# Attention with pooled queries, two MLPs on one core: row sums inverted in PSUM, a weight's sign added as a signed zero, transfers of a pair spread over its steps

## Chip, core and metric

The kernel runs on one core of a Trainium2 chip. The metric is the time of one execution on the device in microseconds, as the median of several runs. The core has TensorE (matrix products and transposes), VectorE, ScalarE and GpSimd for elementwise work, and SyncE, which here issues most of the transfers; 16 DMA engines move the data. In rows of the profile these are PE, DVE, ACT, POOL and SP.

## What is computed

```python
def _attn_ref(q, k, v):                      # batch 2, heads 8, seq 1152, head_dim 64
    q_pool = q.reshape(B, H, S // 2, 2, D).mean(axis=3)
    scores = scale * np.matmul(q_pool, k.transpose(0, 1, 3, 2))
    scores = scores - np.max(scores, axis=-1, keepdims=True)
    attn = np.exp(scores)
    attn = attn / (np.sum(attn, axis=-1, keepdims=True) + 1e-09)
    return np.matmul(attn, v).astype(np.float32)
...
x = np.ascontiguousarray(attn_out.transpose(0, 2, 1, 3)).reshape(B * S, H * D)   # 1152 x 512
x = _moe_ref(x=x, **moe_kwargs)              # (h * tanh(softplus(h))) @ w_out, h = x @ w_in, 512 -> 2048 -> 512
return _moe2_ref(x=x, **moe2_kwargs)         # 8 experts 512 -> 1024 -> 512, ReLU, weighted by 8 Sinkhorn rounds
```

The weights `w_in` and `w_out` of the first MLP arrive as float64, read as int64; all else is float32. Products are made of two float32r parts, high and low, of each operand.

## The kernel before

Three stages follow each other: attention (0 to about 265 us), the first MLP, and the experts. The change is in the first.

**Attention** goes through 8 pairs of heads. Each pair has 9 tiles of 128 query rows, so there are 72 steps `g` in one loop, and `p, t = divmod(g, 9)` gives the pair and the place `t` in it (0 to 8). In step `g`, TensorE makes the scores of tile `g` into the single PSUM tile `psS` (6 matmuls; 12 at place 4, whose tile holds rows of both heads, from `qz`). VectorE takes them out with a running minimum (L483). ScalarE makes the exponentials with their row sum (L497). SyncE copies the exponentials of tile `g - 1` into a buffer `er` of another type, 576 KB (`hand_over`, L503); there are two such buffers. TensorE transposes tile `g - 3` out of `er` in 9 transposes of 128x128 (`psT`, L560); ScalarE (L563) and VectorE (L566) split the result into high and low parts `eth` and `etl`; and TensorE multiplies them with V (`psA`, L581). The PSUM pool `ps_t` has four buffers in turn; `psT`, `psk`, `psq` and `psr` share them.

What else happens in a pair, by tables and lists in the code:

- `TURN` says at which place the transposes of K (`psk`) and Q (`psq`) are made for the next or the same pair. Q comes in three parts: u = 0 at place 6 for the next pair, u = 1 at place 1 and u = 2 at place 0. After each, `swap` has SyncE copy one half of the partitions to the other (`qT`, 2 x 128 KB, or `qz`, 2 x 64 KB). Part u = 2 is first read by the scores of place 4, u = 1 by those of place 5.
- `row_sums` at place 0 of the next pair adds 1e-9 to the 128x9 row sums and inverts them on VectorE; `turn_sums` at place 1 transposes them to 9x128 (`psr`), VectorE copies them out (`rt`, L515), SyncE writes them to DRAM (`row`, L520) and reads them back with a broadcast in three transfers (`rx`, L526). GpSimd multiplies the finished sums with `rx` (L607).
- The list `first` holds what SyncE must issue at the start of the next step, ahead of that step's `hand_over`. Each engine and SyncE work off their instructions in order, so a transfer that waits holds up what is behind it.
- GpSimd's queue loads and splits q, k and v (`prep`).
- `load_w` prepares the weights of the MLP. Six tiles of 128x512 float64 values (512 KB each, `raw`) are prepared within attention, marked `busy`; each is planned at five times `ts` counted in steps `g`. SyncE loads `raw` 2.4 stages of 2 steps ahead of `ts[0]`; there the high words are scaled by 2^-112 on GpSimd (L149) and the low words converted on ScalarE (L153). VectorE shifts and masks each half of a tile (L160) at `ts[1]` and two steps later, and puts the sign into it (L169) one step after each. GpSimd then joins high and low word (L175) and splits the result.

## Time and profile before

| | |
|---|---|
| median of 3 runs | 1220.34 us (1220.3 to 1220.45) |
| the profiled execution | 1223.26 us |
| its span, first to last instruction | 1221.5 us |
| busy in the span: TensorE, VectorE, ScalarE, GpSimd | 1203.7, 855.8, 592.1, 654.0 us |
| busy share of TensorE | 99% |
| granted TensorE clock | 1.000 (full speed) over the span |

The busy time of an engine is the time in which the profile shows an instruction on it; matmuls are pipelined and their ends are modelled, so that short waits of TensorE may be seen as busy. The time of an execution is a little longer than its span, and an execution under the profiler a little longer than one without.

### The profile page before, as it was taken

The numbers are of one execution on the slowest core, as the hardware profiler recorded it, in microseconds if no ns is written. First come the engines' busy times: TensorE is split into PE (matmuls) and PEld (weight loads), VectorE is DVE, ScalarE is ACT, GpSimd is POOL, SyncE is SP. The second block draws the span as 40 slices with busy tenths as digits, with TensorE's granted clock in tenths as the row PEclk, the third lists the DMA queues.
The fourth block names the chain that finished last, engine by engine and source line by source line (L and its number), as shares of the span: only waits on it lengthen the run. The fifth ranks groups of instructions, "written<-read, shape, count | busy, mean of one in ns | idle before, by whom it ended". The sixth has DMA issues, their size and how long they took to land.

```text
span 1221.5 us, 19362 instructions
## 1 busy us (share of the span) xinstructions
PE 1203.7 (99%) x6840; PEld 1110.4 (91%) x6840; DVE 855.8 (70%) x1598; ACT 592.1 (48%) x1354; POOL 654.0 (54%) x752
## 2 busy tenths in 40 slices
PE   8899999999999999999999999999999999999998
PEld 8899999999999999898888889999888889999887
DVE  7899999876444333787866677766866777866865
ACT  7888889877544443543332233333333233333331
POOL 7667777415444331485755566555555565555551
PEclk9999999999999999999999999999999999999999
DMA  6787787653223210011111111111011111111112
GB/s 202 265 281 263 272 264 255 232 179 120 88 71 98 74 31 30 1 52 53 32 38 45 52 48 49 52 52 52 23 40 52 53 44 52 53 52 38 37 39 78
DMA packets 51985, 116.39 MB, mean 95 GB/s; under 512 B 7977, under 2 KB 22897, under 8 KB 51889
## 3 DMA queue, kind: packets, MB, share of 16 engines
q1 hardware_dynamic: 48400, 103.36, 25.9%
q0 software_dynamic: 3488, 11.80, 3.3%
q8 instruction: 54, 0.88, 0.3%
q14 instruction: 43, 0.34, 0.1%
HBM read 66.86 MB, written 2.40 MB: 57 GB/s over the span
## 4 chain that ended last, share of the span: by engine, by line
PE 90%; DVE 5%; DMA 4%; ACT 1%; issue 1%; POOL 0%; POOLq 0%; ACTq 0%
PE po L1237 30%; PE c L1067 26%; PE ph L231 10%; PE po L806 8%; PE psS L478 4%; PE psA L581 4%; DMA er<-e 4%; PE psT L560 3%; DVE e L483 2%; DVE etl L566 1%; PE psk L410 1%; PE psw L646 0%; ACT eth L563 0%; PE pg L861 0%; PE psq L456 0%
## 5 line engine op out<-in xcount | busy, mean ns | idle before, releaser
L83 POOL TENSOR_TENSOR wslotsl<-s,wslotsh 128x256 fp32r<-128x256 f32 x180 | 132.0, 743 | 237.1 <-ACT wslotsh L76 237.1
L1245 DVE SCALAR_TENSOR_TENSOR oacc<-po,Pm,oacc 128x512 f32<-128x512 f32 (+1 forms) x217 | 161.1, 746 | 102.2 <-PE po L1237 95.8
L1237 PE MATMUL po<-wdbl,hhall 128*128 128x512 f32 (+1 forms) x543 | 214.4, 395 | 0.0
L1237 PE MATMUL po<-wdbh,hlall 128*128 128x512 f32 (+1 forms) x543 | 214.1, 394 | 0.0
L1237 PE MATMUL po<-wdbh,hhall 128*128 128x512 f32 (+1 forms) x543 | 214.0, 394 | 0.0
L1084 ACT ACTIVATE t<-c 128x384 f32<-128x384 f32 x80 | 39.3, 491 | 246.2 <-PE c L1067 246.2
L1104 ACT ACTIVATE hhall<-c 128x384 fp32r<-128x384 f32 x180 | 88.6, 492 | 127.4 <-DVE c L1100 124.7
L1237 PEld LDWEIGHTS po<-wdbh,hhall 128*128 128x128 f32 x543 | 102.1, 188 | 24.3
L1237 PEld LDWEIGHTS po<-wdbl,hhall 128*128 128x128 f32 x543 | 102.1, 188 | 23.3
L1237 PEld LDWEIGHTS po<-wdbh,hlall 128*128 128x128 f32 x543 | 102.1, 188 | 23.2
L83 POOL TENSOR_TENSOR wslotsl<-rawu,wslotsh 128x256 fp32r<-128x256 f32 x120 | 90.9, 772 | 49.8 <-ACT wslotsh L76 49.8
L483 DVE TENSOR_SCALAR_CACHE_REDUCE e<-psS 128x1152 f32<-128x1152 f32 x72 | 97.3, 1352 | 22.0 <-PE psS L478 11.7
L566 DVE TENSOR_TENSOR etl<-psT,eth 128x384 fp32r<-128x384 f32 (+1 forms) x240 | 108.0, 507 | 4.8 <-ACT eth L563 4.2
L563 ACT ACTIVATE eth<-psT 128x384 fp32r<-128x384 f32 (+1 forms) x240 | 92.8, 477 | 15.6 <-PE psT L560 15.2
L1105 DVE SCALAR_TENSOR_TENSOR hlall<-c,hhall 128x384 fp32r<-128x384 f32 x180 | 98.7, 548 | 2.1
L1067 PE MATMUL c<-x2l,wslotsh 128*128 128x384 f32 x280 | 94.3, 337 | 0.0
L1067 PE MATMUL c<-x2h,wslotsl 128*128 128x384 f32 x280 | 94.1, 336 | 0.0
L1067 PE MATMUL c<-x2h,wslotsh 128*128 128x384 f32 x280 | 93.8, 335 | 0.0
L497 ACT ACTIVATE e<-e,nm 128x1152 f32<-128x1152 f32 x70 | 89.3, 1276 | 0.1
L175 POOL TENSOR_TENSOR wt<-wt,raw 128x512 int32<-128x512 int32 x32 | 42.4, 1325 | 84.0 <-DVE wt L169 59.8
L478 PE MATMUL psS<-kT,qT 128*128 128x384 f32 x384 | 81.9, 348 | 2.8 <-DVE e L483 2.7
L76 ACT ACTIVATE wslotsh<-s 128x256 fp32r<-128x256 f32 x180 | 72.0, 411 | 24.3 <-DVE s L1033 24.3
(365 smaller groups left out, 3117.2 us busy)
## 6 DMA issues: line engine op xcount, KB each, us to landing
er<-e SPq DMA_DIRECT2D x70, 576.0 KB, 4.1
rawd<-in_moe_w_dram SPq DMA_DIRECT2D x60, 256.0 KB, 2.7
rawu<-in_moe_w_dram SPq DMA_DIRECT2D x30, 384.0 KB, 3.3
raw<-in_moe_w_in_dram SPq DMA_DIRECT2D x16, 512.0 KB, 4.3
raw<-in_moe_w_out_dram SPq DMA_DIRECT2D x16, 512.0 KB, 3.7
vraw<-in_v_dram POOLq DMA_DIRECT2D x15, 288.0 KB, 4.7
kraw<-in_k_dram POOLq DMA_DIRECT2D x13, 288.0 KB, 4.6
qT<-qT SPq DMA_DIRECT2D x28, 128.0 KB, 3.1
```

Of the source, the lines that this page charges most:

```text
L83: eng.tensor_tensor(out=lo, in0=src, in1=hi.bitcast(F32), op=ALU.subtract)
L231: nc.tensor.matmul(ps[:, 0:TH], lhsT=a, rhs=b, start=(n == 0), stop=(n == len(ops) - 1))
L478: nc.tensor.matmul(ps[:, kb, 0:TH], lhsT=a, rhs=kt[:, kb * TH:(kb + 1) * TH], start=(n == 0), stop=(n == len(ops) - 1))
L483: nc.vector.tensor_scalar(sc, ps[:, :, 0:TH], -1.0, None, op0=ALU.mult, op1=ALU.min, accum_out=nm)
L497: nc.scalar.activation(e, sc, AF.Exp, bias=nm, scale=-1.0, accum_out=rsS[p][:, t:t + 1])
L563: nc.scalar.activation(eh[:, cs, o:o + b - a], ps[:, 0:3, a:b], AF.Copy)
L566: nc.vector.tensor_tensor(out=el[:, cs, o:o + b - a], in0=ps[:, 0:3, a:b], in1=eh[:, cs, o:o + b - a].bitcast(F32), op=ALU.subtract)
L806: nc.tensor.matmul(ps[:, 0:TH], lhsT=a, rhs=b, start=(n == 0), stop=(n == len(ops) - 1))
L1067: nc.tensor.matmul(cb[c], lhsT=a_, rhs=b_, start=FIRST[n] and m == 0, stop=LAST[n] and m == len(ops) - 1, skip_group_check=True)
L1105: los.append(lambda: nc.vector.scalar_tensor_tensor(out=lo, in0=b, scalar=0.0, in1=hi.bitcast(F32), op0=ALU.max, op1=ALU.subtract))
L1237: nc.tensor.matmul(ps[:, 0:w], lhsT=a, rhs=b[:, cs], start=(n == 0), stop=(n == len(ops) - 1))
L1245: nc.vector.scalar_tensor_tensor(out=oa, in0=ps[:, 0:w], scalar=gate, in1=oa, op0=ALU.mult, op1=ALU.add)
```

## The change

Four things are edited, all in attention.

1. `row_sums` goes. `turn_sums` transposes the raw sums; VectorE adds 1e-9 to them in PSUM, in place, and a reciprocal takes them from PSUM to `rt`, on 9 partitions of 128 elements.
2. For the six `busy` tiles GpSimd writes, just ahead of its scaling, a second product of the high words with 2^-112 twice into the tile `wt`: a zero that has the word's sign. The shift (L160) combines the shifted word with it by OR, where it took a mask by AND, and the sign's own instruction (L169) is left out for these tiles.
3. The swaps of Q's parts 1 and 2 and the broadcasts of `rx` (but for the last pair) are put into `first` twice, so that they go out a step later. Part 0 of Q is transposed first in its step.
4. The `busy` tiles are loaded 11 steps ahead of `ts[0]` in place of 4.8.

```diff
@@ load_w, plan64
             def scale(x):
                 if x and busy:
+                    box["t"] = wpools["t"].tile([P, GF], U32, tag="wt", name=f"wt{which}_{i}_{u}")
+                    nc.gpsimd.tensor_scalar(
+                        box["t"].bitcast(F32), box["h"], 2.0 ** -112, 2.0 ** -112, op0=ALU.mult, op1=ALU.mult)
                     nc.gpsimd.tensor_scalar(box["h"], box["h"], 2.0 ** -112, 0.0, op0=ALU.mult, op1=ALU.add)
...
                 if busy:
                     nc.vector.scalar_tensor_tensor(
-                        out=box["t"][:, cs], in0=h, scalar=3, in1=mask.to_broadcast(list(h.shape)),
-                        op0=ALU.logical_shift_left, op1=ALU.bitwise_and)
+                        out=box["t"][:, cs], in0=h, scalar=3, in1=box["t"][:, cs],
+                        op0=ALU.logical_shift_left, op1=ALU.bitwise_or)
...
-            at(ts[0] - 2.4 * stage, "dma", dma)
+            at(ts[0] - (11 if busy else 2.4 * stage), "dma", dma)
...
                 at(ts[1] + 2 * j, "dve", lambda cs=cs: shift(cs))
-                at(ts[1] + 2 * j + parts - 1, "dve", lambda cs=cs: sign(cs))
+                if not busy:
+                    at(ts[1] + 2 * j + parts - 1, "dve", lambda cs=cs: sign(cs))
...
@@ trans_q
-            first.append(lambda: swap(t))
+            first.append((lambda: swap(t)) if u == 0 else lambda: first.append(lambda: swap(t)))
...
-        def row_sums(p):
-            rs = rsS[p]
-            nc.vector.tensor_tensor(out=rs, in0=rs, in1=eps.to_broadcast([P, QTL]), op=ALU.add)
-            nc.vector.reciprocal(rs, rs)
-
         def turn_sums(p):
...
-            nc.vector.tensor_copy(rt, ps[0:QTL, 0, :])
+            sums = ps[0:QTL, 0, :]
+            nc.vector.tensor_scalar(sums, sums, EPS, None, op0=ALU.add)
+            nc.vector.reciprocal(rt, sums)
...
             def out():
                 nc.sync.dma_start(out=row, in_=rt)
-                first.append(back)
+                first.append(back if p == NPAIR - 1 else lambda: first.append(back))
...
@@ turn
-                    fs.append(lambda pp=pp, u=u: trans_q(pp, u))
+                    fs.insert(0 if u == 0 else len(fs), lambda pp=pp, u=u: trans_q(pp, u))
...
-            if p and t == 0:
-                row_sums(p - 1)
```

SyncE's queue in pair 1 before, from the hand-over of tile 9 (its place 0) on. `er9` is the buffer of tile 9, `qT1_1` part 1 of Q, `raw0_0_0` the first load of weights:

```order
L503 DMA er9_705<-e9_610 128x1152
L450 DMA qT1_1_683<-qT1_1_683 64x512 x2
L520 DMA row0_722<-rt0_720 9x128
L503 DMA er10_766<-e10_672 128x1152
L526 DMA rx0_723<-row0_722 64x576
L526 DMA rx0_723<-row0_722 64x512
L526 DMA rx0_723<-row0_722 64x64
L503 DMA er11_825<-e11_734 128x1152
L141 DMA raw0_0_0_838<-in_moe_w_in_dram 128x512
L503 DMA er12_879<-e12_792 128x1152
```

The same stretch of the queue now:

```order
L503 DMA er9_699<-e9_608 128x1152
L450 DMA qz1_137<-qz1_137 64x256 x2
L517 DMA row0_717<-rt0_714 9x128
L503 DMA er10_761<-e10_666 128x1152
L450 DMA qT1_1_677<-qT1_1_677 64x512 x2
L503 DMA er11_819<-e11_729 128x1152
L523 DMA rx0_718<-row0_717 64x576
L523 DMA rx0_718<-row0_717 64x512
L523 DMA rx0_718<-row0_717 64x64
L503 DMA er12_874<-e12_786 128x1152
L503 DMA er13_930<-e13_848 128x1152
L139 DMA raw0_0_1_946<-in_moe_w_in_dram 128x512
```

The swap of qz, which stood ahead of `er9`, now stands behind it, that of qT behind `er10`, the broadcasts behind `er11`, and the load behind `er13`; it is that of the second tile.

The first tile is loaded in pair 0. There SyncE's queue now reads (before, the row with `raw` was not there):

```order
L503 DMA er4_426<-e4_364 128x1152
L139 DMA raw0_0_0_448<-in_moe_w_in_dram 128x512
L503 DMA er5_485<-e5_397 128x1152
L450 DMA qT1_0_465<-qT1_0_465 64x512 x2
L503 DMA er6_549<-e6_457 128x1152
```

One load thus moved from the fourth step of pair 1 to the sixth step of pair 0, ahead of three hand-overs there.

VectorE at places 0 and 1 of pair 2 before. `e18` and `e19` are the scores of places 0 and 1, `wt0_0_0` the first weight tile, `rs1` the row sums of pair 1, `xs1` sums of pair 1:

```order
L483 TENSOR_SCALAR e18_1108,nm18_1109<-psS18_1101 128x1152
L160 SCALAR_TENSOR_TENSOR wt0_0_0_1111<-raw0_0_0_838,mask_74 128x256
L566 TENSOR_TENSOR etl1_2_1027<-psT15_0_1119,eth1_2_1026 128x3x128
L566 TENSOR_TENSOR etl1_2_1027<-psT15_1_1125,eth1_2_1026 128x3x128
L566 TENSOR_TENSOR etl1_2_1027<-psT15_2_1131,eth1_2_1026 128x3x128
L598 TENSOR_TENSOR xs1_1024<-psA1_1_1089,avt1_1_1148 64x320
L507 TENSOR_TENSOR rs1_655<-rs1_655,eps_137 128x9
L508 RECIPROCAL rs1_655<-rs1_655 128x9
L483 TENSOR_SCALAR e19_1168,nm19_1169<-psS19_1161 128x1152
L169 SCALAR_TENSOR_TENSOR wt0_0_0_1111<-raw0_0_0_838,wt0_0_0_1111 128x256
...
L515 COPY rt1_1217<-psr1_1215 9x128
```

The same places of VectorE now:

```order
L483 TENSOR_SCALAR e18_1107,nm18_1108<-psS18_1100 128x1152
L161 SCALAR_TENSOR_TENSOR wt0_0_0_1052<-raw0_0_0_448,wt0_0_0_1052 128x256
...
L595 TENSOR_TENSOR xs1_1021<-psA1_1_1088,avt1_1_1146 64x320
L483 TENSOR_SCALAR e19_1162,nm19_1163<-psS19_1155 128x1152
L563 TENSOR_TENSOR etl1_3_1176<-psT16_0_1177,eth1_3_1175 128x3x128
L563 TENSOR_TENSOR etl1_3_1176<-psT16_1_1183,eth1_3_1175 128x3x128
L563 TENSOR_TENSOR etl1_3_1176<-psT16_2_1189,eth1_3_1175 128x3x128
L511 TENSOR_SCALAR psr1_1208<-psr1_1208 9x128
L512 RECIPROCAL rt1_1210<-psr1_1208 9x128
```

The add and the reciprocal of 128x9 left place 0, the sign left place 1, and an add and a reciprocal of 9x128 stand where the copy stood.

## Rows read from the trace of the kernel before

**Rows 1.** Stretch of attention: its length, then busy time (instructions) of each engine.

```profile
0.00:265.00 265.00, 251.54 (x1929) 240.42 (x1930) 232.12 (x483) 226.81 (x504) 168.70 (x191) 1.00 0.74 250
```

**Rows 2.** TensorE's waits: engine, line, for whom; total us, times, longest.

```profile
PE psT L560 <- DMA er<-e: 7.6, 8, 2.0
```

**Rows 3.** Timeline of TensorE: start, length, instructions, idle time before them.

```profile
22.68 0.93 PE L560 MATMUL psT<-identr,er 128*128 128x128 f32 x9 [0.53 <-DMA er<-e]
...
36.62 0.94 PE L560 MATMUL psT<-identr,er 128*128 128x128 f32 x9 [1.03 <-DMA er<-e]
...
59.67 0.51 PE L560 MATMUL psT<-identr,er 128*128 128x128 f32 x4 [1.96 <-DMA er<-e]
...
107.93 1.17 PE L560 MATMUL psT<-identr,er 128*128 128x128 f32 x9
...
113.57 2.38 PE L478 MATMUL psS<-kT,qz 128*128 128x384 f32 x12
116.40 0.93 PE L560 MATMUL psT<-identr,er 128*128 128x128 f32 x9 [0.45 <-DMA er<-e]
...
216.85 0.93 PE L560 MATMUL psT<-identr,er 128*128 128x128 f32 x9 [1.67 <-DMA er<-e]
```

**Rows 4.** Chain that ended last, pair 7: start, us to the next link.

```profile
242.48 2.11 PE psS L478 x12
```

**Rows 5.** Timeline of SyncE's queue in pair 3: start and length of the issue.

```profile
105.90 1.55 SPq L450 DMA_DIRECT2D qT<-qT  x2
...
109.16 0.48 SPq L503 DMA_DIRECT2D er<-e  x1
112.02 1.75 SPq L526 DMA_DIRECT2D rx<-row  x3
113.88 0.53 SPq L503 DMA_DIRECT2D er<-e  x1
114.45 0.61 SPq L141 DMA_DIRECT2D raw<-in_moe_w_in_dram  x1
```

**Rows 6.** Stretches; last two columns DMA share, GB/s. Pair 0; pair 3, places 4-6.

```profile
28.00:32.00 4.00, 3.51 (x28) 3.29 (x27) 3.25 (x9) 3.98 (x12) 2.56 (x3) 1.00 1.00 312
116.38:120.33 3.95, 3.36 (x27) 3.21 (x28) 3.18 (x6) 2.99 (x7) 0.65 (x1) 1.00 0.95 381
120.33:123.54 3.21, 3.19 (x27) 3.18 (x28) 2.76 (x5) 2.86 (x6) 3.04 (x4) 1.00 0.66 266
123.54:126.59 3.05, 3.05 (x30) 3.01 (x29) 2.77 (x5) 2.77 (x6) 2.96 (x4) 1.00 0.44 183
```

**Rows 7.** VectorE's groups by form: count, total us, mean ns, idle before.

```profile
L169 DVE SCALAR_TENSOR_TENSOR wt<-raw,wt 128x256 uint32<-128x256 uint32 x12 | 7.7, 644 | 0.0
...
L515 DVE COPY rt<-psr 9x128 f32<-9x128 f32 x8 | 2.2, 270 | 0.0
...
L508 DVE RECIPROCAL rs<-rs 128x9 f32<-128x9 f32 x8 | 1.7, 216 | 0.3
...
L507 DVE TENSOR_TENSOR rs<-rs,eps 128x9 f32<-128x9 f32 x8 | 1.6, 206 | 0.0
L900 DVE RECIPROCAL crec<-psk 128x8 f32<-128x8 f32 x8 | 1.6, 199 | 0.5 <-PE psk L899 0.5
...
L884 DVE COPY nmx<-psb 128x1 f32<-128x1 f32 x1 | 0.1, 144 | 0.0
```

**Rows 8.** Timelines of GpSimd and VectorE in pairs 3 and 5.

```profile
105.22 1.44 POOL L83 TENSOR_TENSOR kst<-kraw,kst 128x576 fp32r<-128x576 f32 x1
106.00 0.94 DVE L169 SCALAR_TENSOR_TENSOR wt<-raw,wt 128x256 uint32<-128x256 uint32 x1
...
170.32 0.42 DVE L169 SCALAR_TENSOR_TENSOR wt<-raw,wt 128x256 uint32<-128x256 uint32 x1
```

**Rows 9.** GpSimd: a group of its instructions, and one of its timeline, pair 3.

```profile
L149 POOL TENSOR_SCALAR raw<-raw 128x512 f32<-128x512 f32 x6 | 3.9, 658 | 0.0
...
119.68 1.40 POOL L607 TENSOR_TENSOR xs<-xs,rx 128x576 f32<-128x576 f32 x1 [5.47 <-DVE xs L598]
```

More of the change, by code (lines that the diff above doesn't have):

```diff
@@ L68, in pool_attention_mish_sinkhorn_kernel @@
     nc.vector.tensor_copy(identr, ident)
-    mask = const.tile([P, 1], U32, name="mask")
-    nc.vector.memset(mask, 0x7FFFFFF8)
     ones = const.tile([P, P], F32, name="ones")
@@ L325, in pool_attention_mish_sinkhorn_kernel @@
         wpools["t"] = pool("wt", 2)
-        eps = tiny.tile([P, 1], F32, tag="eps", name="eps", bufs=1)
-        nc.vector.memset(eps, EPS)
         qz = []
@@ L336, in pool_attention_mish_sinkhorn_kernel @@
         loader = nc.sync
-        loads, first = [], []
+        first = []
         def heads(p):
@@ L721, in pool_attention_mish_sinkhorn_kernel @@
             pre = turn(p, t) if g < NQ else []
-            waiting = first + loads
-            first[:], loads[:] = [], []
+            waiting, first[:] = list(first), []
             for f in waiting:
```

## The prediction

> **What bounds the kernel now.** The profiled execution took 1223.26 us, 1.8 us more than its span and 2.9 us above the median of the three timed runs (1220.34 us); I make the sum against 1223.26 and carry the difference over to the median. First the stretches [rows 1]: TensorE is occupied in 251.5 of the first 265 us, so some 13.5 us of it are open there; everything that the diff edits is issued in these 265 us. Behind them TensorE is the bound without a gap worth naming, and time saved in attention comes off the end one for one.
>
> Which gaps? The waits of TensorE [rows 2] name one kind above all: the transposes psT wait for the handed-over row `er`, 8 times, 7.6 us. The timeline of TensorE [rows 3] places them: 0.53 and 1.03 us in pair 0 and at its end, and six from 59.67 to 216.85 us, which leaves 7.6 - 0.53 - 1.03 = 6.0 us. The reader is to see that the recorded idle is too small: the 12 score matmuls at 113.57 start 2.83 us before the transposes that follow them, with 0.45 of it recorded as idle, while the same 12 take 2.11 us on the chain where nothing is late [rows 4]. So a stall is worth its idle time and about 0.27 us, and six are worth 6.0 + 1.6 = 7.6 us. They all lie at places 4 to 6 of a pair, and each waits for a row handed over two steps before (a place is a step's number in its pair, 0 to 8).
>
> Why is `er` late there? The queue of SyncE in pair 3 [rows 5]: the swap of qT goes out at 105.90, in front of the hand-over at 109.16; the three broadcasts of rx go out from 112.02 on, directly ahead of the hand-over at 113.88; and 512 KB of weights follow at 114.45. The DMA engines are 0.95 busy at place 4, but 0.66 and 0.44 at places 5 and 6 [rows 6]. The transfers of a pair fit; they stand too close together at places 1 to 4.
>
> **The change, part by part.** *Swaps and broadcasts a step later, weights at place 5.* Behind the hand-over at place 1 there is now only the small swap of qz, so the hand-over of place 2 no longer has the 256 KB swap of qT in front of it; rx no longer stands in front of the hand-over of place 3; and 512 KB leave place 3. The later consumers have room: qT is read at place 5, two steps after its new issue, and qz at place 4, also two steps after. rx is read by GpSimd at the end of the pair's sums, where GpSimd had sat idle 5.47 us waiting for VectorE [rows 9]; about one step later is about when it is wanted, so this may cost GpSimd up to a microsecond, which is idle time there. Queued behind the waiting row and rx transfers on SyncE is the next hand-over, but it waits for a free `er` buffer, until the transposes of its own step, anyway. Bounds of the gain: 7.6 us if all six stalls go; 3 us if only half of the recorded idle does, since the same bytes must still pass. I take 6.5, near the upper end, because at places 5 and 6 there are 0.34 x 3.21 + 0.56 x 3.05 = 2.8 us of free DMA time [rows 6] and 512 KB take 0.524 MB / 312 GB/s = 1.7 us by the rate of the stretch from 28 to 32 us, the one with a share of 1.00. Term: **-6.5 us**.
>
> *Where the weights land instead.* The first of the six loads now goes out at place 5 of pair 0, a little after the transposes at 22.68 us [rows 3]. Just behind it lies that stretch with all 16 DMA engines busy [rows 6], and the hand-over at its end is the one that already comes 1.03 us late at 36.62 [rows 3]. The load's 1.7 us come on top, less what idle shares around the stretch absorb: bounds 0 and 1.7, taken 1.2. The other five fall on the free time worked out above: bounds 0 and 0.5 each, taken 0.4 in all. Term: **+1.6 us**.
>
> *The sign.* On VectorE the twelve L169 instructions go, 7.7 us together [rows 7]; the twelve shifts stay, with the tile as second operand in place of the mask. GpSimd gets six more instructions of the kind of L149, 0.66 us each [rows 9], 4 us in its idle time.
>
> *The row sums.* At place 0 an add and a reciprocal of 128x9 go: 1.6 + 1.7 us over eight pairs. At place 1 the copy of 9x128 from PSUM (0.27 us) becomes an add there, which I price alike, and a reciprocal of 9x128 comes. No row shows one of 128 elements in a lane. From below: the copy of the same shape, 0.27 us. From above: the reciprocal of 8 elements from PSUM takes 199 ns and the copy of one element 144 ns, so 55 ns / 7 = 7.9 ns for each further element, and 144 + 127 x 7.9 = 1.15 us. I take 1.15: it is worked out from the same operation, and the copy isn't. So 8 x 1.15 = 9.2 us come and 7.7 + 3.3 = 11.0 go: VectorE gains 1.8 us in all, but not where it counts. TensorE follows VectorE at places 0 to 2 through the four buffers of ps_t: the fourth tile after psr takes psr's buffer, and the nine transposes at 107.93 take 1.17 us, where the nine at 116.40, whose buffers are long free, take 0.93 [rows 3]. In pairs 2 to 6 L169 at place 1 (0.64 us on the mean, 0.94 in pair 3) goes and the reciprocal takes its place: even. In pairs 1 and 7 no L169 stood at place 1, and psr comes free some 0.8 us later, of which I count 0.5 each. Place 3, where the other L169 stood, is bound by the twelve score matmuls. Bounds for the two edits: -2 us (a cheap reciprocal) and +3; taken **+1.0 us**.
>
> *The transposes of q first at place 6*: the same instructions in another order; ScalarE copies qT before the first eth instead of after the last, and the swap behind it has a step. Nothing is counted; should qst be late, TensorE would wait there.
>
> Sum: -6.5 + 1.6 + 1.0 = -3.9 us: 1223.26 becomes 1219.4 in a profiled execution, and 1220.34 becomes **1216.4 us** as a median.
>
> *A rule against the sign's part.* L169 at 106.00 took 0.94 us while GpSimd's subtraction, begun at 105.22, ran until 106.66; at 170.32 it took 0.42 [rows 8]. The Trainium skill (SBUF — State Buffer, Who interferes with whom) has it that a VectorE instruction with two SBUF inputs and a GpSimd instruction that reads SBUF exclude each other, the later one standing still until the earlier is done; these two rows agree. By that rule every GpSimd instruction that moves later can hold a shift of VectorE, and the added one makes E below the forecast; by the two rows alone a meeting is as likely lost as won, and I count nothing.
>
> **The rivals.** *A, the forecast*: 1216.4 (own range 1213 to 1218.6), chance 0.60.
> *B, the reciprocal is cheap*: the last term is -2, the sum -6.9, 1213.4. For it: nothing but the copy's row. Chance 0.15.
> *C, the stalls only move*: the bytes are the same, and `er` comes late at places 7 and 8 and in pair 0 instead. Gain 3, cost 1.7 and 0.3 for each of five loads, 1.0 for VectorE: +1.2 us, 1221.5, or with less of the cost 1220.3, as before. For it: a share of 0.95 at place 4 that is not the weights' alone. Against: the shares of 0.66 and 0.44 behind it [rows 6]. Chance 0.15.
> *D, slower: the reciprocal holds up TensorE*. Place 1 of each pair; psr's buffer comes free 1.15 us later and TensorE loses all of it, 9.2 us in eight pairs: -6.5 + 1.6 + 9.2 = +4.3, 1224.6. It decides from (6.5 - 1.6) / 8 = 0.6 us lost in a pair. Against: in five of the pairs L169 makes room. Chance 0.05.
> *E, GpSimd's later work holds the shift.* From pair 3 on GpSimd works without a gap from place 4 to place 0; 0.66 us more there puts its subtraction further over VectorE's shift at place 0, as with L169 in [rows 8]: 0.66 us in each of pairs 3 to 6, 2.6 us. -3.9 + 2.6 = -1.3, 1219.0. Chance 0.05.
>
> **How the numbers follow.** No change means within 0.2%, 2.4 us, about what a measurement of this kernel can tell: 1217.9 to 1222.8. Faster: 0.53 of A's 0.60, and B's 0.15: 0.68. Within: the rest of A (0.07), C but for 0.01 (0.14), and E (0.05): 0.26. Slower: D and 0.01 of C: 0.06. The range goes down to B's edge (all six stalls gone, half of pair 0's cost: -7.6 + 0.6 + 0.4 - 2 = -8.6, 1211.7) and up past E to the nearer half of C, 1220.4.
>
> **What would show it.** Right: waits of psT for `er` under 2 us after 40 us; the first load on SyncE between the hand-overs of pair 0, and the one stall at its end longer; L169 gone from VectorE's places 1 and 3. Reciprocals of 9x128 near 1.15 us; under 0.4 is B. D would be nine transposes at place 2 that take over 1.7 us. C would be stalls at places 7 and 8. Wrong altogether would be the forecast if `er` is late at places 4 to 6 as before: then it is the loads of q, k and v on GpSimd's queue, which don't move.

## The result, and the profile after

The changed kernel is slower: 1234.31 us in the median of four runs (1233.12 to 1238.61) against 1220.32 us (1218.06 to 1220.45); the ratio is 1.0125, 95% interval 1.0098 to 1.0152. Forecast was 1216.4.

The profiled execution took 1234.62 us, 1232.7 of it span: 11.2 us more span than in [rows 1]'s execution. Two marks divide these 11.2 us, the first matmul of the MLP (`ph`) and the first of the experts' up projection (`c`). Timeline of TensorE of the changed kernel (start, length, instruction):

```profile
271.78 0.42 PE L233 MATMUL ph<-xh,wul 128*128 128x384 f32 x1
...
533.32 0.34 PE L1061 MATMUL c<-x2h,wslotsl 128*128 128x384 f32 x1
```

and of the kernel before:

```profile
264.77 0.42 PE L231 MATMUL ph<-xh,wul 128*128 128x384 f32 x1
...
524.11 0.34 PE L1067 MATMUL c<-x2h,wslotsl 128*128 128x384 f32 x1
```

Attention ends 7.0 us later. From ph to c it takes 261.54 for 259.34 us, from c to the end of the span 699.38 for 697.39: another 4.2 us, in stages that the diff doesn't touch. (The medians differ by 14 us and the spans by 11.2, because the profiled execution of before lay 2.9 us above its median.)

TensorE's waits in attention, which answer to [rows 2]:

```profile
PE psq L456 <- DVE etl L563: 5.3, 3, 2.0
PE psT L557 <- DMA er<-e: 4.5, 5, 2.2
PE psS L478 <- DVE e L483: 3.1, 5, 1.5
```

The waits for `er` did fall, from 7.6 to 4.5 us, but a new line stands above them: the transposes of Q at place 0 wait for VectorE. VectorE's groups of instructions by line, which answer to [rows 7]:

```profile
L161 DVE SCALAR_TENSOR_TENSOR wt<-raw,wt 128x256 uint32<-128x256 uint32 x12 | 18.6, 1549 | 0.0
...
L512 DVE RECIPROCAL rt<-psr 9x128 f32<-9x128 f32 x8 | 7.6, 946 | 0.3
```

The reciprocal costs 0.95 us, near the 1.15 of the estimate. The shift L161, 12 x 0.42 us where nothing disturbs it, takes 18.6 us. Where, the timelines of pair 4's place 0 show, VectorE first, then GpSimd:

```profile
135.51 1.36 DVE L483 TENSOR_SCALAR_CACHE_REDUCE e<-psS 128x1152 f32<-128x1152 f32 x1 [0.42 <-PE psS L478]
...
136.79 3.04 DVE L161 SCALAR_TENSOR_TENSOR wt<-raw,wt 128x256 uint32<-128x256 uint32 x1
139.76 1.47 DVE L563 TENSOR_TENSOR etl<-psT,eth 128x384 fp32r<-128x384 f32 x3
```

```profile
135.46 1.44 POOL L388 TENSOR_TENSOR qraw<-qraw 128x576 f32<-128x576 f32 x1
136.85 0.68 POOL L78 TENSOR_SCALAR vst<-vraw 128x576 fp32r<-128x576 f32 x1
137.50 0.67 POOL L390 TENSOR_SCALAR qraw<-qraw 128x576 f32<-128x576 f32 x1
138.14 1.41 POOL L81 TENSOR_TENSOR vst<-vraw,vst 128x576 fp32r<-128x576 f32 x1
139.84 0.59 POOL L347 DMA_DIRECT2D vraw<-in_v_dram  x1 [0.30 <-POOL vst L81]
```

The shift starts at 136.79 and ends at 139.83: just when GpSimd, after four instructions without a gap, pauses to issue a transfer. In pairs 2 to 6 it takes 1.06, 2.17, 3.04, 3.69 and 3.78 us at place 0, and place 0 as a whole 4.07, 5.16, 6.04, 6.69 and 6.78 us where it had 3.73, 4.04, 3.73, 4.74 and 4.10. (Here and below a place lasts from the start of its L483 on VectorE to the start of the next one, and a pair from its first L483 to that of the next pair.)

The wait for rx shows in GpSimd's timeline of pair 2 and in the transfer of rx (KB, us from issue to landing):

```profile
91.54 1.41 POOL L604 TENSOR_TENSOR xs<-xs,rx 128x576 f32<-128x576 f32 x1 [7.92 <-DMA rx<-row]
```

```profile
rx<-row SPq DMA_DIRECT2D x1, 128.0 KB, 8.0
```

The product starts 21.4 us into the pair, where it started after 18.6.

Pair 0 takes 29.52 for 27.71 us. The transposes at its end, 1.03 us late in [rows 3], are now 2.2 us late, and then the granted clock falls. TensorE's timeline, then stretches with its busy time, granted clock, DMA share and GB/s:

```profile
33.38 1.35 PE L557 MATMUL psT<-identr,er 128*128 128x128 f32 x9 [2.21 <-DMA er<-e]
```

```profile
28.00:32.00 4.00, 2.69 (x21) 1.00 0.98 303
32.00:36.00 4.00, 2.62 (x15) 0.66 0.94 309
36.00:40.00 4.00, 4.00 (x30) 0.91 0.38 152
```

The clock was at its upper level (2.4 GHz) all through the profiled execution of before; here part of 32 to 40 us runs at the lower one (1.2 GHz).

My theory after this reading: (1) rx a step later makes GpSimd wait at its product with rx (L604), the unbroken run of its instructions behind that ends later, and VectorE's shift is shut out at place 0; (2) taking out two small tiles moved most tiles in SBUF, by 32 bytes as I reckon (the traces hold no addresses), which costs the 4.2 us behind attention; (3) the first weights' load costs 2 to 3 us in pair 0. Rivals: the added instruction on GpSimd or the reciprocal is the cause of place 0; the 4.2 us are clock or chance.

### The profile page after: what moved, and what is told of

It is laid out like the page before. It is cut to its first block, busy times and chain, and to the rows that moved or that the text cites. A ratio compares the mean times of both kernels' runs of the same rounds, so it can differ in the third digit from the quotient of the medians.

```text
span 1232.7 us, 19359 instructions
## 1 busy us (share of the span) xinstructions
PE 1210.4 (98%) x6840; PEld 1115.3 (90%) x6840; DVE 866.5 (70%) x1576; ACT 592.1 (48%) x1354; POOL 656.6 (53%) x758
## 4 chain that ended last, share of the span: by engine, by line
PE 91%; DVE 3%; DMA 3%; ACT 2%; issue 1%; POOL 0%; DVEq 0%; ACTq 0%; POOLq 0%
PE po L1231 30%; PE c L1061 26%; PE ph L233 10%; PE po L800 8%; PE psA L578 5%; PE psS L478 5%; DMA er<-e 3%; PE psT L557 3%; DVE e L483 1%; DVE etl L563 1%; DVE wt L161 1%; ACT e L497 1%; ACT kT L411 1%; PE psk L410 0%; ACT eth L560 0%
## 5 line engine op out<-in xcount | busy, mean ns | idle before, releaser
L483 DVE TENSOR_SCALAR_CACHE_REDUCE e<-psS 128x1152 f32<-128x1152 f32 x72 | 97.0, 1348 | 20.6 <-PE psS L478 15.0
```

The lines of the kernel that those rows point to most:

```text
L483: nc.vector.tensor_scalar(sc, ps[:, :, 0:TH], -1.0, None, op0=ALU.mult, op1=ALU.min, accum_out=nm)
```

## The experiments

Each was timed in five rounds beside the kernel before on the same chip (1218.4 to 1219.7 us there). Executions of one kernel spread by up to 8 us (e13: 1220.2 to 1228.5), and a profile is one of them; so totals are compared by medians, across chips by the ratio to the kernel before on the same chip, and profiles only tell where time lies. The waits for `er` above all differ between executions: in e7, whose attention has the instructions of the kernel before, they are 3.1 us in place of 7.6. Line numbers are as in the prediction; a kernel's own numbers differ by a few.

**e1, the two small tiles put back**

```diff
+    mask = const.tile([P, 1], U32, name="mask")
+    nc.vector.memset(mask, 0x7FFFFFF8)
...
+        eps = tiny.tile([P, 1], F32, tag="eps", name="eps", bufs=1)
+        nc.vector.memset(eps, EPS)
```

> The changed kernel with the two small tiles put back that the change took out (the 128x1 mask and the 128x1 epsilon, written once at the start and never read), so that all later tiles lie at the addresses of the kernel before; no other instruction changes. Theory of addresses: the change moved most tiles by 32 bytes, and this made the matmuls after attention slower, which cost the 4.2 us that came after the first MLP matmul (first ph to first c 262.65 for 260.59 us, first c to the end 694.54 for 692.38). Then this kernel gives about 1230 us, with the first ph matmul still near 272 us and the two stretches back at 260.6 and 692.4. Rival: the 4.2 us have another cause (the clock, or an order that changed); then about 1234 us, and both stretches stay.

(The expectation's stretches are taken from a later c and to the last matmul.) Measured: 1233.64 us, ratio 1.0107 (1.0088 to 1.0127). Its marks, in TensorE's timeline, with a span of 1234.4 us:

```profile
277.50 0.42 PE L235 MATMUL ph<-xh,wul 128*128 128x384 f32 x1
...
537.07 0.34 PE L1065 MATMUL c<-x2h,wslotsl 128*128 128x384 f32 x1
```

ph to c 259.57 us, c to the end 697.33: both stretches are back. The total is not, since attention took 5.7 us more in this execution (pair 0 alone 32.1 us, place 0 of pairs 3 to 5 6.9 us each). The two tiles explain the tail; the median doesn't confirm the 4 us by itself, e7 does.

**e7, the kernel before with two more small tiles**

```diff
     mask = const.tile([P, 1], U32, name="mask")
+    pad = const.tile([P, 1], U32, name="pad")
...
+        pad2 = tiny.tile([P, 1], F32, tag="pad2", name="pad2", bufs=1)
```

> The kernel before with two more small tiles (128x1, written once, never read) next to the mask and the epsilon, so that most tiles lie 32 bytes further, at the same place within 64 bytes as in the changed kernel; nothing else changes. Theory of addresses: the two stretches after attention take 2.1 us more each, as in the changed kernel (first ph to first c 261.5 for 259.3 us, first c to the end 699.4 for 697.4), so about 4 us slower than before. Rival: the 4 us belong to the change's other edits, and e1_pads lost them by chance; then no change.

Measured: 1225.96 us, ratio 1.0060 (1.0042 to 1.0078): 7.3 us slower by two tiles that nobody reads, where 4 were expected. Its marks (span 1224.1 us):

```profile
259.27 0.42 PE L233 MATMUL ph<-xh,wul 128*128 128x384 f32 x1
...
521.05 0.34 PE L1071 MATMUL c<-x2h,wslotsl 128*128 128x384 f32 x1
```

ph to c 261.78 us as in the changed kernel, c to the end 703.05, more than the 699.4 expected. A group of the experts' matmuls by form, between 540 and 1215 us, in the kernel before, the changed kernel and e7:

```profile
L1067 PE MATMUL c<-x3h,wslotsl 128*128 128x384 f32 x38 | 12.7, 333 | 0.0
```

```profile
L1061 PE MATMUL c<-x3h,wslotsl 128*128 128x384 f32 x38 | 12.7, 335 | 0.0
```

```profile
L1071 PE MATMUL c<-x3h,wslotsl 128*128 128x384 f32 x38 | 12.9, 340 | 0.0
```

Each matmul takes 2 to 7 ns more, with the clock at 1.00. So the two tiles cause the tail's loss; that it is their 32 bytes, and that e7 lies where the changed kernel does, is not shown, and the two differ (335 and 340 ns). In all kernels here that have the two small tiles of before and no more (before, e1 to e6, e8 to e17) the stretches are 259.3 to 259.9 and 697.3 to 698.1 us; only the changed kernel and e7 stand outside. Which tiles meet badly was not tried.

**e2, e3, e4: one part undone each, on e1**

e2 (rx as before):

```diff
-                first.append(back if p == NPAIR - 1 else lambda: first.append(back))
+                first.append(back)
```

> As e1_pads, but the broadcasts of the row sums (rx) are issued one step earlier, as in the kernel before; the swaps stay a step later. Theory: GpSimd's product with rx waits for a broadcast that comes a step later, and its unbroken run then lies over VectorE's shift at place 0, which took 1.06 to 3.78 us in pairs 2 to 6. With rx earlier the run ends some 1.7 us earlier, the shift there takes under 2.2 us each, and the time falls by 4 to 7 us against e1_pads. Rival: the run is late because of the six added instructions on GpSimd or the order of its work alone; then the shift still takes 2 to 4 us and the time falls by less than 1.5 us. Second rival: the er transfers are again held up at places 4 to 6 by rx, which gives back up to 2 us of it.

e3 (sign on VectorE again):

```diff
-                    nc.gpsimd.tensor_scalar(
-                        box["t"].bitcast(F32), box["h"], 2.0 ** -112, 2.0 ** -112, op0=ALU.mult, op1=ALU.mult)
...
+                at(ts[1] + 2 * j + parts - 1, "dve", lambda cs=cs: sign(cs))
```

> As e1_pads, but the weights' sign is again made by VectorE (shift with the mask, then the second instruction, twelve of each), and GpSimd makes no signed zero. Theory: GpSimd's run is 0.66 us shorter in pairs 2 to 6, so the shift at place 0 is let in 0.66 us or more earlier; the sign instructions (0.64 us each) lie elsewhere and cost up to 0.3 us each: 1 to 3 us faster than e1_pads. Rival: VectorE's 7.7 us of sign instructions are on the path; then 0 to 3 us slower than e1_pads.

e4 (row sums before the turn again):

```diff
+            nc.vector.tensor_copy(rt, ps[0:QTL, 0, :])
...
+            if p and t == 0:
+                row_sums(p - 1)
```

> As e1_pads, but the epsilon and the reciprocal of the row sums are again taken at place 0 from the 128x9 tile, before the turn. Theory: the reciprocal of 9x128 in PSUM (0.95 us) delays place 1 of pairs 1 and 7 by 0.9 and 1.2 us and no other; without it 1.5 to 2.5 us faster than e1_pads, less the 0.42 us that the two small instructions take at place 0: 1 to 2 us faster. Rival: place 1 is no longer bound by VectorE, so within 0.7 us of e1_pads.

Measured: 1232.09, 1230.99 and 1232.19 us, ratios 1.0105, 1.0091 and 1.0098: none undoes the loss, all within 3 us of e1. e3 and e4 gain what was expected of them, if anything (the intervals are 2 us wide to either side); e2 gains 1.5 us where 4 to 7 were expected. The shift's group in e2:

```profile
L163 DVE SCALAR_TENSOR_TENSOR wt<-raw,wt 128x256 uint32<-128x256 uint32 x12 | 6.2, 514 | 0.0
```

With rx on time the shift at place 0 takes 0.42 us in every pair, so the first theory's mechanism stands. But the time didn't follow: that is the second rival, with a price beyond its 2 us. TensorE's waits in e2:

```profile
PE psT L561 <- DMA er<-e: 12.6, 8, 2.4
```

With place 0 short, the waits for `er` are 12.6 us; they are 6.1 in e1. The later swap and rx now go out together between two hand-overs, as in e10 below. In e4 the epsilon's instruction, which reads two SBUF tiles, is shut out at place 0 as well (7.2 us for eight).

**e5, the shift where GpSimd stands idle, on e1**

```diff
-                at(ts[1] + 2 * j, "dve", lambda cs=cs: shift(cs))
+                at(ts[1] + (1 if busy else 2) * j, "dve", lambda cs=cs: shift(cs))
...
-        load_w(0, 0, [(t, t + 2, t + 7, t + 8, t + 9) for t in evenly(16, 9)], 2, parts=2, busy=True)
+        load_w(0, 0, [(t, t + 6, t + 8, t + 8, t + 9) for t in evenly(16, 9)], 2, parts=2, busy=True)
```

> As e1_pads, but VectorE's two shifts of a weight tile stand at places 4 and 5, where GpSimd stands idle (it waits for rx there, 8.4 us in pair 4 of e1_pads), in place of places 0 and 2; GpSimd's join of the tile follows a place later. No instruction is added or left out. Theory of the lock: at place 0 the shift, which reads two tiles in SBUF, can't start while GpSimd's unbroken run lasts; in the gap every shift takes 0.42 us and place 0 falls from 4.2 to 6.9 us to 3.5, which is 10 to 14 us off the attention of e1_pads, so the time is 1220 to 1224 us. Rival: place 0 is long because what GpSimd makes late (the splits of k and v) is late for TensorE or VectorE there too; then place 0 stays over 5 us and the time is within 4 us of e1_pads.

Measured: 1226.40 us, ratio 1.0069 (1.0053 to 1.0084), 4.6 us under e1 by the ratios (7.2 by the medians, but on another chip), not the 10 to 14 expected. Its shift and its waits:

```profile
L163 DVE SCALAR_TENSOR_TENSOR wt<-raw,wt 128x256 uint32<-128x256 uint32 x12 | 6.9, 575 | 0.0
```

```profile
PE psT L561 <- DMA er<-e: 9.0, 10, 2.4
```

Place 0 is 3.5 to 3.9 us now. Ending the shut-out was worth about a third of e1's loss of 13; part of the rest came back as waits for `er` (9.0 us for 6.1 in e1), among them at places 4 and 5.

**e6, the first weights' load as late as before, on e1; e8, three remedies**

```diff
-            at(ts[0] - (11 if busy else 2.4 * stage), "dma", dma)
+            at(ts[0] - ((4.8 if t[0] == 16 else 11) if busy else 2.4 * stage), "dma", dma)
```

> As e1_pads, but the first weight tile is loaded as late as in the kernel before (4.8 steps ahead, in pair 1), the five others in step 5 as in the change. Theory: that load makes er late at places 7 and 8 of pair 0, and the stall lets TensorE's granted clock fall (0.60 from 33 to 37 us in e1_pads); without it pair 0 takes 27.7 to 28.3 us in place of 32.1 with the clock at 1.00 throughout: 2 to 4 us faster than e1_pads. Rival: the stall there comes from the k and v loads and the er transfers alone; then pair 0 stays over 29.5 us and the time within 1 us.

Measured: 1233.15 us, ratio 1.0115 (1.0098 to 1.0133), no gain. Pair 0 takes 26.3 us, less than the 27.7 expected; pair 1 takes 35.4, with 6.7 and 4.3 us at places 5 and 6. The stall went with the load, which the kernel before also issues in pair 1 (32.6 us there, 5.0 at place 5).

e8 is e5 and e6 together, with the row sums of e4 and the epsilon as a constant:

```diff
+            nc.vector.tensor_scalar(rs, rs, EPS, None, op0=ALU.add)
+            nc.vector.reciprocal(rs, rs)
```

> As e1_pads, with three remedies together: the shifts at places 4 and 5, the first weight tile loaded as late as before, and the epsilon and the reciprocal taken from the 128x9 tile before the turn (the epsilon as a constant, so that the instruction reads one tile in SBUF and not two). Theory: the shift's 10 to 14 us, pair 0's 2 to 4 us, and 0.5 us at place 1 of each pair come off e1_pads' 1233.6: 1212 to 1218 us, faster than the kernel before. Rival: each remedy uncovers the next wait (er at places 4 to 6 above all); then 1219 to 1224 us.

Measured: 1225.76 us, ratio 1.0061 (1.0046 to 1.0077): the rival, a little above its range. Waits for `er` 10.0 us. The constant was no remedy either: place 0 takes 5.1 us in pairs 3, 5 and 6, since the epsilon, with one input in SBUF now, is shut out too. VectorE and GpSimd in e8, pair 3:

```profile
103.91 1.44 DVE L511 TENSOR_SCALAR rs<-rs 128x9 f32<-128x9 f32 x1
```

```profile
103.89 1.43 POOL L83 TENSOR_TENSOR vst<-vraw,vst 128x576 fp32r<-128x576 f32 x1
```

**e9 to e11, e14, e15: each part of the change alone, on the kernel before**

e9 (rx a step later):

```diff
-                first.append(back)
+                first.append(back if p == NPAIR - 1 else lambda: first.append(back))
```

> The kernel before with one part of the change alone: the broadcasts of the row sums (rx) a step later, save those of the last pair. Theory: this alone makes GpSimd wait at its product with rx, its unbroken run ends 4 to 5 us later, VectorE's shift at place 0 is shut out for 2 to 4 us in each of pairs 2 to 6, and the loads of q, k and v that GpSimd issues come later too: 5 to 9 us slower than before. Rival: the sign on GpSimd and the reciprocal in PSUM are needed for the loss; then within 2 us of before, and the shift at place 0 under 1.5 us each.

Measured: 1233.12 us, ratio 1.0100 (1.0086 to 1.0114): this one line costs 12.2 us by the ratio (10.5 to 13.9), more than the 5 to 9 expected and most of what the whole change costs (15.3). Pair 2 shows how it begins. SyncE's queue, the transfer of rx (KB, us from issue to landing) and GpSimd's timeline in e9:

```profile
82.88 0.59 SPq L141 DMA_DIRECT2D raw<-in_moe_w_in_dram  x1
83.58 2.15 SPq L526 DMA_DIRECT2D rx<-row  x3
```

```profile
rx<-row SPq DMA_DIRECT2D x1, 128.0 KB, 7.2
```

```profile
83.37 0.60 POOL L347 DMA_DIRECT2D vraw<-in_v_dram  x1 [0.30 <-POOL vst L83]
91.98 1.39 POOL L607 TENSOR_TENSOR xs<-xs,rx 128x576 f32<-128x576 f32 x1 [8.01 <-DMA rx<-row]
```

The same three of the kernel before:

```profile
80.07 1.77 SPq L526 DMA_DIRECT2D rx<-row  x3
```

```profile
rx<-row SPq DMA_DIRECT2D x1, 128.0 KB, 4.5
```

```profile
87.77 1.42 POOL L607 TENSOR_TENSOR xs<-xs,rx 128x576 f32<-128x576 f32 x1 [5.06 <-DVE xs L598]
```

Before, the product waited for VectorE's sums, and the 128 KB of rx had landed at 85.1, 2.7 us earlier. In e9 rx goes out behind a hand-over and 512 KB of weights, with v's 288 KB issued just ahead of it, and takes 7.2 us in place of 4.5. The stretches of its issue, in e9 and in the kernel before (columns: length; busy time of TensorE, its weight loads, VectorE, ScalarE, GpSimd; granted clock; DMA share; GB/s):

```profile
81.90:85.72 3.82, 3.82 (x29) 3.68 (x28) 3.10 (x7) 2.98 (x8) 1.77 (x2) 1.00 1.00 344
```

```profile
80.07:84.60 4.53, 4.53 (x38) 4.39 (x36) 3.78 (x9) 3.56 (x8) 2.26 (x3) 1.00 0.99 308
```

The DMA engines are full in both, so their share doesn't tell the two apart; what was issued ahead of rx does. The weights alone aren't it: in the changed kernel they go out later, rx stands behind a hand-over with v's load beside it, and takes 8.0 us. Which transfer ahead holds it was not tried. The product starts 21.5 us into its pair, where it was 18.6, and the 9.6 us of GpSimd's work that begin with it and have no gap move along, towards the next pair's place 0. Two losses follow, and a pair shows one or the other: in pairs 3 and 4 VectorE is shut out (L160 2.98 and 1.96 us, then the epsilon 1.66 and 1.67 us; place 0 is 7.8 and 6.8 us), in pairs 1 and 5 `er` is late at place 5 (5.4 and 5.3 us, where the kernel before had 5.0 and 3.4), and the step behind it takes 4.0 and 4.5 us for 3.0 and 3.2, in pair 5 at a granted clock of 0.75 to 0.83.

e10 (the swaps a step later):

```diff
-            first.append(lambda: swap(t))
+            first.append((lambda: swap(t)) if u == 0 else lambda: first.append(lambda: swap(t)))
...
-                    fs.append(lambda pp=pp, u=u: trans_q(pp, u))
+                    fs.insert(0 if u == 0 else len(fs), lambda pp=pp, u=u: trans_q(pp, u))
```

> The kernel before with one part of the change alone: the turn of the first q tile first in its step, and the swaps of the second and third tile a step later; rx, the weights' loads, the sign and the row sums as before. Theory: rx left where it was, GpSimd is on time and no shift is shut out (0.42 to 0.5 us at place 0); the er stalls (7.6 us before) change by 2 us at most either way: 0 to 3 us faster than before. Rival: the later swaps hit er at places 3 and 4; then 1 to 4 us slower.

Measured: 1224.33 us, ratio 1.0035 (1.0020 to 1.0050): the rival's price, with `er` late at places 4 and 5 in place of 3 and 4. SyncE's queue and TensorE's timeline in pair 2, and the stretches of TensorE around it:

```profile
76.62 0.48 SPq L503 DMA_DIRECT2D er<-e  x1
77.14 1.64 SPq L450 DMA_DIRECT2D qT<-qT  x2
78.88 2.56 SPq L526 DMA_DIRECT2D rx<-row  x3
81.55 0.53 SPq L503 DMA_DIRECT2D er<-e  x1
```

```profile
88.50 1.02 PE L560 MATMUL psT<-identr,er 128*128 128x128 f32 x9 [1.98 <-DMA er<-e]
```

```profile
84.00:88.00 4.00, 2.51 (x19) 1.00 1.03 328
88.00:92.00 4.00, 3.50 (x20) 0.65 0.82 317
```

The swap of 256 KB left the place ahead of one hand-over and stands, together with rx, ahead of the next: 4.2 us of issue between two hand-overs. The waits for `er` are 10.2 us in this execution, the slowest of seven, and the clock is down behind the stall (0.65).

e11 (the sign from GpSimd):

```diff
+                    nc.gpsimd.tensor_scalar(
+                        box["t"].bitcast(F32), box["h"], 2.0 ** -112, 2.0 ** -112, op0=ALU.mult, op1=ALU.mult)
...
-                at(ts[1] + 2 * j + parts - 1, "dve", lambda cs=cs: sign(cs))
+                if not busy:
+                    at(ts[1] + 2 * j + parts - 1, "dve", lambda cs=cs: sign(cs))
```

> The kernel before with one part of the change alone: the weights' sign as a signed zero from GpSimd, without VectorE's second instruction. Theory: 0.66 us more on GpSimd's run and 1.3 us less on VectorE per pair; with rx on time the shift at place 0 is shut out for 1 us at most: within 2 us of before. Rival: those 0.66 us alone push the run over the shift, 2 us or more at place 0 of each pair, and it is 5 us or more slower.

Measured: 1223.12 us, ratio 1.0030 (1.0018 to 1.0043). Place 0 went as the rival said; the total, 3.7 us, lies between theory and rival. VectorE's timeline in pair 4, and TensorE's longest waits:

```profile
131.13 2.06 DVE L163 SCALAR_TENSOR_TENSOR wt<-raw,wt 128x256 uint32<-128x256 uint32 x1
...
134.91 1.66 DVE L511 TENSOR_TENSOR rs<-rs,eps 128x9 f32<-128x9 f32 x1
```

```profile
PE psS L482 <- DVE e L487: 7.5, 9, 1.5
PE psr L517 <- DVE rs L512: 1.7, 5, 0.4
```

Place 0 is 6.4 to 7.2 us in pairs 2 to 6, and there is no wait for `er` left at all. Place 0 takes 13.9 us more in these five pairs than in the profile of before, the pairs as a whole 4.3: 4.4 us come back at place 1, which L169 has left, and 5.3 at places 3 to 6. I read the latter so that a stall at place 0 gives the transfers time to catch up; that is argued, not shown, since pair 1, whose place 0 is as short as before (3.6 us), has lost its wait for `er` too.

e14 (epsilon and reciprocal in PSUM) and e15 (weights in step 5):

```diff
-            nc.vector.tensor_copy(rt, ps[0:QTL, 0, :])
+            sums = ps[0:QTL, 0, :]
+            nc.vector.tensor_scalar(sums, sums, EPS, None, op0=ALU.add)
+            nc.vector.reciprocal(rt, sums)
```

> The kernel before with one part of the change alone: epsilon and reciprocal in PSUM after the turn. Theory: place 1 grows by 0.4 to 0.9 us (4.4 us where nothing else stands there), place 0 loses 0.4 us: within 3 us of before, on the slower side. Rival: place 0 is freed of two instructions that wait for GpSimd, and it is 2 to 4 us faster.

```diff
-            at(ts[0] - 2.4 * stage, "dma", dma)
+            at(ts[0] - (11 if busy else 2.4 * stage), "dma", dma)
```

> The kernel before with one part of the change alone: the six weight tiles loaded 11 steps ahead. Theory: the load moves from place 3 to place 5, behind the er transfers that are late at places 4 to 6, but the first stands in pair 0, whose er stalls grow by 2 to 4 us: within 3 us of before. Rival: er at places 4 to 6 gains all of the 512 KB that go: 2 to 5 us faster.

Measured: e14 1225.99 us, ratio 1.0046 (1.0029 to 1.0064), more than expected: places 0 and 1 together take 8.7 to 8.8 us in pairs 2 to 6 for 7.8 to 7.9, 1.0 us a pair. (L169 still stands at place 1 here; the change takes it away.) e15 1223.74, ratio 1.0022 (1.0007 to 1.0038): pair 0 takes 32.0 us, pairs 2 to 6 together 158.3 for 160.6: within the 3 us expected.

**e12, e13, e16, e17: is there something to keep?**

e12 is e1 with rx and the loads as before and the row sums as in e8; the later swaps and the sign remain.

```diff
-                first.append(back if p == NPAIR - 1 else lambda: first.append(back))
+                first.append(back)
...
-            at(ts[0] - (11 if busy else 2.4 * stage), "dma", dma)
+            at(ts[0] - (4.8 if busy else 2.4 * stage), "dma", dma)
```

> As e1_pads, but rx a step earlier and the weights' loads 4.8 steps ahead, both as before, and the epsilon as a constant and the reciprocal on the 128x9 tile before the turn; of the change the later swaps and the sign on GpSimd are left. Theory: what was measured as dear (rx, the early load, the reciprocal in PSUM at place 1 with 4.4 us) is out, 7.7 us of sign instructions are off VectorE: 1214 to 1219 us, no slower than before. Rival: GpSimd's longer run or the swaps still cost; then 1221 to 1226 us.

Measured: 1226.10 us, ratio 1.0046 (1.0031 to 1.0061): the rival; `er` 9.7 us. e13 is e11 with the shifts in GpSimd's idle time and the epsilon as a constant:

```diff
-            nc.vector.tensor_tensor(out=rs, in0=rs, in1=eps.to_broadcast([P, QTL]), op=ALU.add)
+            nc.vector.tensor_scalar(rs, rs, EPS, None, op0=ALU.add)
...
-        load_w(0, 0, [(t, t + 2, t + 7, t + 8, t + 9) for t in evenly(16, 9)], 2, parts=2, busy=True)
+        load_w(0, 0, [(t, t + 5, t + 7, t + 8, t + 9) for t in evenly(16, 9)], 2, parts=2, busy=True)
```

> As e11 (the kernel before with the weights' sign from GpSimd), but VectorE's shifts stand at places 3 and 4, where GpSimd stands idle, and the epsilon is a constant, so that VectorE has nothing at place 0 that reads two tiles in SBUF. Theory of the lock alone: place 0 falls from 6.4 to 7.2 us in e11 to 3.7 and nothing else grows, 13 us less: 1207 to 1212 us. Rival, the er transfers as the next bound: with place 0 short, er of place 2 is again late at places 4 to 6, 6 to 9 us in all in place of none in e11, and the time is 1215 to 1220 us.

Measured: 1222.81 us, ratio 1.0027 (1.0012 to 1.0043), a little above the rival's range. Its waits:

```profile
PE psT L564 <- DMA er<-e: 6.8, 8, 1.5
```

Place 0 is 3.6 to 3.9 us, and the waits for `er` are back, from none in e11. Nothing stands ahead of `er` here that didn't before: with place 0 short, `er` is the next bound here, as in e2 and e5.

e16 keeps five of the six loads of e15 and leaves the first where it was; e17 does the same to e13.

```diff
-            at(ts[0] - 2.4 * stage, "dma", dma)
+            at(ts[0] - (11 if busy and t[0] > 16 else 2.4 * stage), "dma", dma)
```

> The kernel before with the weight tiles loaded 11 steps ahead save the first, which keeps its 4.8. Theory: pair 0 as in the kernel before, and 2 us less in pairs 2 to 6, since 512 KB have gone from the full transfer engines of places 3 to 5: 1 to 3 us faster than before. Rival: the 2.3 us of one profiled execution were chance; then within 1 us of before.

> As e13 (sign from GpSimd, shifts at places 3 and 4, epsilon as a constant), with five of the six weight tiles loaded 11 steps ahead. Theory: place 0 stays at 3.6 to 3.9 us and the er stalls of e13 (6.8 us) fall by half: 3 us less than e13's 1222.8, so 1218 to 1221 us. Rival: what sets the pair's time is the sum of the transfers, wherever they stand; then within 1 us of e13.

Measured: e16 1219.04 us, ratio 0.9999 (0.9987 to 1.0010); e17 1221.39, ratio 1.0009 (0.9997 to 1.0021). e16 is its rival, no gain; e17 lies 2.2 us under e13 by the ratios, between its theory and its rival, and its constant epsilon is shut out once for 3.15 us (place 0 of pair 4). In the profile of e16 the waits for `er` are 2.3 us and the span 1215.2, but the median is that of before: the profile is of its shortest execution. No kernel here beats the kernel before.

## Why the prediction was wrong

**The sentence that failed** is the one on rx: "about one step later is about when it is wanted, so this may cost GpSimd up to a microsecond, which is idle time there". I took the issue a step later for a landing a step later, and the idle time for room. rx had 2.7 us to spare in pair 2, less than a step; behind the transfers that now go out ahead of it, it takes 7.2 us to land (e9) and 8.0 (changed kernel) where it took 4.5, though the DMA engines were as full before. The product, which had waited for VectorE's sums, now waits for rx, 3 us longer, and with it move the 9.6 us of work that it begins in an in-order queue. Idle time ahead of an instruction is no room when what stands behind it is due. Alone this edit costs 12.2 us. Undone alone (e2) it ends the shut-out at place 0 but brings back 1.5 us or less; the later swap and rx then stand together ahead of one hand-over.

**Rival E had the mechanism and a wrong price.** It counted the 0.66 us of the added instruction in four pairs, 2.6 us, with a lock that costs one GpSimd instruction. Measured is the shift at place 0 with 13.7 us in five pairs, where 2.1 would do. Both factors were off: GpSimd is late by 3 us because of rx, and VectorE waits for the end of GpSimd's run, not of one instruction. The added instruction alone, with rx on time, already takes place 0 to 6.4 to 7.2 us (e11); in e2, with the same instruction and longer waits for `er`, it doesn't. (That a place 0 that has grown delays rx in its own pair, and so the next place 0, fits the growth from pair 2 to 6, but was not tried.)

**The term of -6.5 us** rested on the queue order: less ahead of the hand-overs of places 2 and 3. In the changed kernel the waits for `er` did shrink: of the 4.5 us left 2.2 lie in pair 0, 1.3 at places 4 to 6, where they were 6.0, and 1.0 at place 7. But the swaps alone (e10) cost 4.3 us, with 10.2 us of these waits, and the one kernel in which they vanish (e11) has a long place 0. So I think that they shrank because TensorE and VectorE were held up elsewhere; that is argued. What is left at place 7 and in pair 0 is rival C; the larger stall moved to place 0, and there it costs more. Part of the 6.0 may also have been chance: e7, with the same instructions in attention, has 3.1 us in all, and then the term, sized on one execution, was too large from the start. The prediction's own condition ("if `er` is late at places 4 to 6 as before: then it is the loads of q, k and v on GpSimd's queue") is met by e5 and e13, where place 0 is short; but five loads of weights at place 5 on the kernel before leave 2.3 us of waits (e16), and that q, k and v are the cause was not tried.

**+1.6 us for the weights**: e15 gives 2.7 us (0.9 to 4.6), in pair 0 as forecast; the fall of the clock behind the stall (0.50 from 36 to 40 us in e15) was not in the term. **+1.0 us for sign and row sums** was mis-sized: alone they cost 3.7 us (e11: 2.2 to 5.2) and 5.6 us (e14: 3.5 to 7.8). The sign's part was put at nothing, and its shut-out is what e11 shows. For the row sums the reading was right and the size small: the reciprocal takes 0.95 us for the 1.15 of the estimate, and L169 does make room for it. Where L169 is gone and nothing is shut out (e2), places 0 and 1 together take 7.9 to 8.0 us in pairs 2 to 6 for 7.8 to 7.9, and 7.9 and 7.7 us in pairs 1 and 7 for 7.1 and 6.9: some 2.5 us in all. e14 costs more because L169 stays there.

**Not seen at all**: the diff removes two tiles of 4 bytes a partition, and the addresses of others move. 4.2 us of the loss lie in stages without one edited line; e1 undoes them and e7 makes them.

The single parts come to 12.2 + 4.3 + 3.7 + 5.6 + 2.7 = 28.5 us by their ratios, and 4.2 for the addresses, where the whole change costs 15.3: they overlap. Sign and row sums do, as just said; a stall at place 0 that lets `er` catch up would be another reason. How the sum divides between the parts when they act together is not settled; e1 to e4 only show that no single undoing brings it back.

## To carry to other kernels

A transfer that is moved lands later by more than its issue if other transfers now go out ahead of it: read in the trace how much time it had to spare, what is issued ahead of it and beside it, and ask which in-order engine waits for it and what comes behind on that engine. Where two resources take turns as the bound of a loop (here `er` and place 0), removing one stall is worth little until the other is gone, and adding one is cheap until it is the longer. Waits read from one execution can be twice those of another; see a second one before sizing a gain by them. After an edit that adds or drops a tile, compare the untouched stages too: two small tiles alone were worth 4 to 8 us here.

## What the hardware showed that was not expected

A VectorE instruction with two SBUF inputs (0.42 us) lasted up to 3.78 us beside GpSimd instructions that follow each other without a gap, and was let in when GpSimd paused. The Trainium skill (SBUF — State Buffer, Who interferes with whom) says that whoever issues first has the shared ports for the whole instruction. These runs agree that the two exclude each other (0.42 us in e2, where they don't meet), and add that the waiting engine isn't served between two instructions of the other. The epsilon's add with two SBUF inputs took 1.66 us beside such a run and 0.15 without one (e11). With a constant and one SBUF input it still took up to 1.44 us in e8 and 3.15 us in e17 beside GpSimd, for 0.15 alone.

Two small tiles more or fewer, and so other addresses, made matmuls with 384 columns a few ns longer each (340 ns in one group of e7 and 335 in the changed kernel for 333) at a granted clock of 1.00.

A wait of TensorE of about 2 us was followed by a granted clock of 0.65 to 0.66 over 4 us in some places (pair 0 after, pair 2 in e10) and by none in others (59.67 in [rows 3]: 1.96 us, clock 1.00).

A reciprocal of 9x128 from PSUM took 946 ns, one of 128x9 in SBUF 216.
